# Ninth key blocks of two P V products multiplied together in 64x64 tiles, with a newly written order of the work

## The chip, the cores and the metric

The kernel runs on one core of a Trainium2 chip. The metric is the device time of one execution in microseconds; three runs of the kernel before took 446.49, 446.68 and 447.13 us, and the median, 446.68, is the time that the change is measured against.

## What is computed

Attention with a threshold, over 8 batches of 8 heads with 576 positions of 64 numbers, and then a feed-forward layer on the 4608 tokens:

```python
scores = scale * q @ k.T                          # per batch and head, 576 x 576
thresh = max(scores, axis=-1) - tau               # tau = 0.02
scores = where(scores >= thresh, scores, -1e9)
attn   = exp(scores - max(scores)); attn /= sum(attn) + 1e-9
x      = (attn @ v), heads side by side           # 4608 x 512
h      = maximum(x @ w1, x @ w2, x @ w3)          # 4608 x 768
out    = h @ w_out                                # 4608 x 512
```

All inputs and outputs are fp32.

## The kernel before

**Tiles.** Four heads of a batch make a quad; there are 16 quads. Within a quad, r = 0 and 1 are its two pairs of heads, and i the head within a pair. A head's 576 positions are cut into four blocks of 128 and a rest of 64. The rests of the two heads of a pair share one chunk, so a quad has nine chunks of 128 queries, and a chunk has two score tiles of 128 x 576, one for each pair. The steps (g, idx) are numbered in the order in which they are worked; batch 7 is split in two parts (SPLIT, line 36), so that its feed-forward layer can begin after the first 256 positions of each head.

**One score tile** goes through these steps, each with a letter:

- S (`scores`, line 287): fp32 matmuls of q and k into a PSUM slot. For the fifth chunk of a quad they are of 64x64 tiles, else of 64x128.
- m (`maximum`): VectorE finds the row maximum. For a *masked* tile (its digit in MASKED, line 24, is 1) it also copies the negated scores to SBUF, so that the slot is free afterwards.
- e (`exponents`): ScalarE. For a masked tile exp, from SBUF; for others a Prelu from PSUM that flattens what lies under the threshold, and frees the slot.
- k or n (`numerators`): the second pass with the row sum, on VectorE (k, comparing and multiplying, two operands in SBUF) for masked tiles, on ScalarE (n, exp) for the others.
- r: the reciprocal of both sums of a chunk, on VectorE; p (twice a chunk): the normalisation to bf16 on GpSimd (POOL in the profile), tile P; t: a transposing DMA on SyncE's queue, which brings P into the quad's tile ptq, keys on the partitions.

**The product P V** (O, `product`, line 366) is made per quad and pair r. Its output is a PSUM slot in which head i of the pair has the partitions 64i to 64i + 63. Five key blocks are summed up: four of 128 keys with V's tile vb, and the ninth one, in which the 64 remaining keys of pair 0 stand on partitions 0 to 63 and those of pair 1 on partitions 64 to 127. To multiply that block over all 128 partitions, the tile vrb (`vrs`, line 219, named vr in the profile) has zeros on the other pair's partitions; six memsets put them there at the start. All products are thus 128x64 tiles, the two heads beside each other in the array. A row of 576 queries is written in two runs, of 512 and 64 columns (each matmul writes within one bank of 512). w (VectorE) or x (ScalarE) copies the sum to the tile xt as bf16. `cast_v` (line 221, letter y, on POOL) makes the bf16 V: one copy of the four blocks and two for the ninth.

**The other work:** T transposes q and k of a later quad on PE, a and c copy them out, q swaps halves on POOL; F and B are the two halves of a feed-forward step on PE, h and v (hidden layer) and u (output) its copies on ScalarE and VectorE, o the store; l loads q, k, v of a later quad, g and z load and cast weights.

**The order is written by hand:** the string ORDER (line 40) holds one letter for each step, and S, T, O and F carry the number of the PSUM slot (0 to 3, two banks each) that they take. `issue` (line 603) reads it. Every engine and SyncE's DMA queue work in the order in which their letters stand; between engines only data and free buffers decide.

Of the kernel before, what the change touches and what calls it, by code (L numbers as in the profile page):

```python
# [12 lines left out]
BF16 = mybir.dt.bfloat16  # L13
AX = mybir.AxisListType.X
AF = bass_rust.ActivationFunctionType
# [6 lines left out]
FLAT = 2.0 ** -100  # L22

MASKED = """
010100101001000000011101001010000001100010001000101000011000100000100000
000011111001100001001001001001000001011100101001000110001010010000010011
000010011101100001001100100001001010001100010111000001000100000110000101
001001001101100000110001000100100100001100100011100111010011010111110110
"""


# [6 lines left out]
PBUFS = 6  # L38

ORDER = """  # L40
lllllmlyelgS2ymylS3emgnlT0mleS1lakS2nlqermS3ylmeS0pmeS1kpS3elmS2nlzmelrmnT1pS0tcnperkT1pameS1zmteS3knpS0rnmp
emS2permeqS1mnqT3meqktepS0ncS2ntrpmS3npretprmeS1pmnS0tpmS3npmS1etpmeS0rT2mnplkeT1akgeS2qmgepmteS3rkpekntS0pe
rrnmT2pncS3ptamepS1meqtrS2meyqnS3lmqeS0pmelpknT1lpS2nmeymeS3lrkepS0tcnT2rpnmS1tpnmaprrmS0eS2pmteS1pmT3epctep
meT3O0ykntnyS2etrykpnO1wnprmaS0xptrS3meS2zmeS1mzgeS0mlnS3pmleS1pmelO2qmelpkteO0nrnklpS3nlwgxprrmS2leS0pmeF3q
tmT1eBqcF0eqkthBpnS2vS1nF3pmnF0pmBerBkepS2vhT1tnprmS0S3apmetS1zmeS2rmpeF3tmF0epBkepF1tnBvBznvS2ghS3rymnF0gmS
1eplBrkepF2tnmF3BnpvBnqvT1S0hprrcT2S3pamS1eymzF2emBeqgkF0etyS3nS1vpnmtF2pBmezBveS3prgnS0mtS1phrmT3epO2metzeF
0wpnS1gcqS2nmBqnmO3zekepgS1xvlF2nS3mtnF0rrmpBeBlpveS1lphS2mntF3zmeBrpS0evS1lpnmF2lnpS3rmleBptmS1nzvS0nS3mtpn
S2rpeF1rmepmtepS0mBepmtekF3ektekT2uBarklpukS0uqlS2urS1mlnS3pmleO0pmlepmelO2wtnkS1xrS0tepmF2myF3eBkepT1tBhcF0
nqvT2T1laByrcynS3qvS2nlqmF1tnpF0meS3pBelmBlhrrF2kpelS1vnBlprF3mnlS0pveBtprmS1hS2pmeS3tpmeS0pmF2emF1eBkeT3Bva
tF0nvqT2T3BkqlaS1nrcS3phmtS2npmF0epF1mteBqkBeqF3lnvS2lnBrvplS0hmtpS1F3meS2mteBrmepS0vnpO1rekpnO3mtnpweS2yrrt  # L50
xS1mF0yymT3epBcnS1pvS2nptF3meS0pmeBomT2hS1okeF0omF3ntBkaBervS1ponrF2vpemS0ptuS3mpeF2metknT1T3rknBparrceS0puS
3mqtuS1mpeS2mpeS3lmF0peomepS1ketqT3S2ncBqnmlqnmlO3ekluktO1urnwperrS0pxS3mptnS2mS1pempS3etmF0peF2meBlkBelS1kh
oF3nrmlF0pnBtvpBerrvS2phlS1mnpS3tmF0peS2mpeBmeF3vF1eoBkntS0vnBS2rmhpS3mepS1mteyF2mF0eyBkteBnrvT3pF1aovT2ynBp
lrcS3hplS0mnyF2lmF1elBykepBlnvT3tS0aS2vnO3rrmtpnmpeS1weptS2mS0prmO3eqtmeqF1eqlT0S2xqcBnlpmS3hlpS0meF2ymF1elB
knlF3vnBokBetS2hvS0nrrF3mpF1mpeBkBpetF2vnprS0uvnT3ptmS2aS1pmeS0trmF3epmnpkeS2tS0ermpBnmopnkS1uS2rurompS0eF3o
mpelmpeS2lkpeS0lmS1elqBmelqmetkO2unktO0erwpurkpT1txT2cS3apF0nmtT1qS2ceBqmnS1yF3hmF2eyrBpeBvptnF0pS1vnBrmtpS3
hS2pmeS0mtS1eF3meF2meBkBeF0knF1vnBBrvhpS3nvT0pF2akyF1tnBmyS0velByrmlS3phS2rlempF1lmyeF0pklBepS3tnvS2nBrmptO1
meprvepS2wnS3plmF0nF1rmepBlkeqS2lBhmtT3nyS0vnS2mqlO1emtpecT2xT0rS3pacF1eqmF2lnyBklqeT0BvlaS3khoS1qnmF0tF2pme
BrBopnvS3teprvF0pnrmS1puS2meS3prmS0epF1tmepmepT2ktBeqncT3tuS0kaS2urqmS3tnpmS1nF0pmemteS3repS1mS2lepmBelykteS
3kuO1rumplnmlpO0ewterpT2xS1cqnoS3mpF0nF2metBkeBkF1hlF3nvBlnrrS0pvlnBpmS2lhS1ymleF0mtS3epBmepF2vF1etkBnS0vnS3  # L60
rmBnpS2rhmpF0emF1pteBkpBerF3vnS2ptvnT0pBramS1pthS0mepF3meqtT2rBecpS1nvylT0ynS2pmlS3amlS1eomS0elO2rmpeomeplO3
ketnwT1F0nctF2xkBnBrvpS1hrF3pmS0qBemqS2onvF1yeF0mBopkeF3tyBnS2vqhBrlrnmpT1S0vaptS2empF1S3mpelBkeplF0vntS2rum
S1pnS0mtepF3rmepmetqS2kS0epBnmmteS1rkepS2lmuS0ulpmS1nlymT3yetF2cekeT3oBrknpamoS0npS3mnS1qtmuO0qurrmqelO2wpel
kpelS0xS3meptF2mS1peBemytF0hrkT3pBecF2nS1vpnS3rymtBpnmS0epS1vlnF3mF2etBmeBkhF0lkeF3nBrvpS1nrvBpnS2mptS0hmpeS
3meF2tmF1eBkeBlrvnT0plS3ravlpS2nlmqF0nlS1mqeBtrrmpF2eS3phBlmepS0tvepS1mS2npS3mepO0meknO1meownT3orxkT2pS0tacF
1nF2qrmeBtpS3evpBmS0tyhF1meT2yBcqoeF3rpkT2F0aptBnvBnS2pvS1hqtmF3nqT0meBrS1npvF2npmT3BactS1ervF3prmS0pueS2omp
F3ekqelmT1ntS0qcnBpmekteS2S1urrmpF0uompekS3eptS2nmS1pnmlO3ermtpekO2pnwS1ykxtyS3emS2BomeyrmepS1rukpS2uoF3meF0
opmnBtykBhpS1ervS2eptmO3pO0mxnS3txS2rmepF0empF1ekBtBevF3hkS2nS0mnBrmF1npF2vepBkBtS0hvO3emO2xkS1xerS3rpmF2mpF
0eF1kpteBnBvpF3BvtBrhkpF2S0vS1prmBptmF3eF0pveBtBhS1vS2mS3mF0F1mBkBF2vhF3keBeO0vnO1kF2kxeBwurS1rvpS0mpS2F3mpe
tmpeS0eoF1mnketBknkBurrupoF2puF0hptF3uvF2pvF1hF0tvF3rvpF2hF1vopF0vF3thF2vF1vF0hoF3vF2ovF1hF0vF3vO2uoO1wF0xF3  # L70
F2hF1vF3vF2hF1vF3vF2hF1vF3vF2hF1vF3vF2hF1vF3vF2hF1vBvF3uuooBF2uuuooo
"""


# [28 lines left out]
def kernel(  # L103
# [34 lines left out]
    one = ctx.enter_context(tc.tile_pool(name="one", bufs=1))  # L138
# [30 lines left out]
    vp = ctx.enter_context(tc.tile_pool(name="vp", bufs=3))  # L169
# [196 lines left out]
    def product(L, r, target, part=None):  # L366

        pt, vb, vrb = L["pt"], L["vb"], L["vrb"]
        st = {}

        runs = {None: ((0, 640, 0, 512), (512, 576, 512, 64)),
                1: ((0, 640, 0, 256),),
                2: ((256, 896, 0, 256), (512, 576, 256, 64))}[part]

        order = [(m, run) for m in range(5) for run in runs] if part is None else \
            [(m, run) for run in runs for m in range(5)]

        def first(where):
            st["ps"] = ps = bank("o", where)
            for m, (*q0, p0, n) in order:  # L380
                for i in range(2):
                    w = vb[:, 2 * r + i, (1, 3, 0, 2)[m], :] if m < 4 else vrb[:, 2 * r + i, :]
                    tensor.matmul(ps[64 * i:64 * i + 64, p0:p0 + n], w,
                                  pt[:, 4 if m == 4 else m + 5 * r, q0[i]:q0[i] + n],
                                  start=(m == 0), stop=(m == 4))

        def on_vector():
            ps = st["ps"]
            dst = target(L["b"])[:, 2 * L["qd"] + r, :]
            if part is None:  # L390
                vector.tensor_copy(out=dst, in_=ps[:, 0:S])
            else:
                vector.tensor_copy(out=dst[:, 256:S], in_=ps[:, 0:320])

        def on_scalar():
            ps = st["ps"]
            dst = target(L["b"])[:, 2 * L["qd"] + r, :]
            if part is None:
                scalar.activation(out=dst, in_=ps[:, 0:S], func=AF.Copy)
            elif part == 1:  # L400
                scalar.activation(out=dst[:, 0:256], in_=ps[:, 0:256], func=AF.Copy)
            else:
                scalar.activation(out=dst[:, 256:S], in_=ps[:, 0:320], func=AF.Copy)
        p = _Piece((L["b"], L["qd"], r, part), first)
        p.vector = on_vector if part != 1 and r == 0 else None
        p.scalar = on_scalar if part == 1 or r == 1 else None
        return p


# [177 lines left out]
    def tiles():  # L587
# [8 lines left out]
    line = {k: [] for k in "menkrptahvuxwcq"}  # L596
# [116 lines left out]
    x = 0  # L713
# [39 lines left out]
```

## Time and profile before

| | |
|---|---|
| runs | 446.49, 446.68, 447.13 us |
| span of the profiled execution, first to last instruction | 445.0 us |
| median of the runs less that span | 1.7 us |
| PE (matmuls) busy, of the span | 95% |
| VectorE (DVE) | 88% |
| ScalarE (ACT) | 89% |
| GpSimd (POOL) | 71% |
| mean TensorE clock granted | 0.992 |
| score tiles, masked ones among them | 288, 105 |

The profile gives no time of its own for the profiled execution beside its span; the 1.7 us are what lies around the span when it is set against the median. In the profile's rows, L91 is the line of the helper that records every operation, so operations are told apart by engine, tile and shape: `o<-ptq,vb 128*64 128x512` is a product's matmul, in an array tile of 128 rows and 64 columns, with 128 x 512 moving numbers. PEld is the loading of weights. Matmul ends are modelled, so the starts carry more than the lengths. SPq is SyncE's DMA queue. "by line" rows are shares of a stretch in the chain of waits.

### The profile page before, as it was taken

What the parts mean: (1) busy time and instruction counts of PE and PEld (TensorE: products, weight loads), DVE (VectorE), ACT (ScalarE), POOL (GpSimd) and SP (SyncE); (2) the same over time, 40 slices, a digit from 0 to 9 for tenths busy, and PEclk for the clock granted to TensorE, in tenths of its full rate; (3) what the DMA queues carried; (4) which work ended last, traced back from release to release, by engine and by line L of the source; (5) the groups of instructions that cost most, each with busy time, mean ns of one, the idle gap of its engine ahead of it and who ended that gap; (6) DMA issues with size and microseconds to landing.
All of it is one profiled execution on the core that took longest, in us unless ns stands there. A gap on an engine that the chain in (4) does not pass through costs nothing.

```text
span 445.0 us, 14089 instructions
## 1 busy us (share of the span) xinstructions
PE 423.6 (95%) x5193; PEld 313.3 (70%) x5193; DVE 393.2 (88%) x1093; ACT 394.4 (89%) x804; POOL 315.9 (71%) x422
## 2 busy tenths in 40 slices
PE   7767799999999999999999999999999999999995
PEld 5434557767787767777687867867687778777772
DVE  4989889999999999989989998999999999989641
ACT  4999999999999999999998999999999999956422
POOL 3998989989686686686768885859767789562300
PEclk9998899999999999999999999999999999999999
DMA  8989999999999978999797999899999979882902
GB/s 251 331 162 213 243 195 234 221 245 229 215 255 195 250 165 175 234 187 228 179 223 170 200 224 182 211 234 199 197 220 202 253 121 173 148 122 34 217 13 108
DMA packets 212773, 87.44 MB, mean 196 GB/s; under 512 B 185824, under 2 KB 199648, under 8 KB 212704
## 3 DMA queue, kind: packets, MB, share of 16 engines
q1 hardware_dynamic: 212000, 85.69, 93.6%
q10 hardware_dynamic: 704, 0.85, 0.6%
q8 instruction: 41, 0.67, 0.6%
q14 instruction: 28, 0.23, 0.2%
HBM read 34.60 MB, written 9.44 MB: 99 GB/s over the span
## 4 chain that ended last, share of the span: by engine, by line
PE 81%; ACT 7%; DVE 6%; issue 4%; POOL 2%; DMA 1%; DVEq 0%; POOLq 0%; ACTq 0%
PE ph L91 30%; PE sc L91 28%; PE po L91 11%; PE o L91 8%; ACT z L91 6%; PE tp L91 4%; DVE z L91 2%; DVE unused L91 2%; DMA qm<-in_q_dram 1%; POOL P L91 1%; DVE hm L91 0%; POOL w L91 0%; ACT qt L91 0%; POOL qs L91 0%; DVE hT L91 0%
## 5 line engine op out<-in xcount | busy, mean ns | idle before, releaser
L91 POOL TENSOR_SCALAR P<-z,rs 128x576 bf16<-128x576 f32 x288 | 228.1, 807 | 85.7 <-DVE rs L91 36.4
L91 PE MATMUL sc<-kt,qt 64*128 64x320 f32 (+2 forms) x640 | 179.1, 429 | 4.9 <-ACT z L91 4.4
L91 PE MATMUL sc<-kt,qs 64*128 64x256 f32 (+2 forms) x640 | 178.6, 418 | 4.7 <-ACT z L91 2.7
L91 PE MATMUL ph<-xt,w 64*128 64x288 bf16 (+2 forms) x2160 | 163.9, 283 | 0.3
L91 PEld LDWEIGHTS <-w 64*128 64x128 bf16 (+1 forms) x2160 | 124.8, 94 | 30.9 <-issue 5.3
L91 DVE TENSOR_SCALAR_CACHE_REDUCE unused<-sc 128x576 bf16<-128x576 f32 x183 | 133.2, 749 | 8.9 <-PE sc L91 8.4
L91 ACT ACTIVATE z<-sc,nm 128x576 f32<-128x576 f32 x183 | 131.3, 740 | 8.5 <-DVE unused L91 5.2
L91 ACT ACTIVATE z<-z 128x576 f32<-128x576 f32 x183 | 123.5, 680 | 0.1
L91 PEld LDWEIGHTS sc<-kt,qs 64*128 64x128 f32 (+1 forms) x640 | 92.4, 178 | 25.3 <-ACT z L91 8.1
L91 PEld LDWEIGHTS sc<-kt,qt 64*128 64x128 f32 (+1 forms) x640 | 92.4, 178 | 19.8 <-ACT z L91 9.3
L91 DVE SCALAR_TENSOR_TENSOR z<-z 128x576 f32<-128x576 f32 x105 | 84.1, 811 | 0.4 <-ACT z L91 0.4
L91 DVE TENSOR_SCALAR_CACHE_REDUCE z<-sc 128x576 f32<-128x576 f32 x105 | 77.7, 752 | 7.4 <-PE sc L91 3.4
L91 ACT ACTIVATE z<-z,nm 128x576 f32<-128x576 f32 x105 | 79.1, 773 | 3.6 <-DVE z L91 3.2
L91 POOL COPY qs<-qt 64x640 f32<-64x640 f32 (+3 forms) x68 | 47.0, 692 | 14.4 <-ACT qt L91 11.0
L91 PE MATMUL po<-wo,hT 64*128 64x512 bf16 (+1 forms) x480 | 54.0, 356 | 0.1
L91 DVE TENSOR_TENSOR hm<-ph,hm 128x576 bf16<-128x576 f32 (+2 forms) x54 | 37.0, 686 | 13.0 <-PE ph L91 11.8
L91 ACT ACTIVATE hm<-ph 128x576 bf16<-128x576 f32 (+2 forms) x54 | 32.1, 594 | 18.4 <-PE ph L91 18.1
L91 PEld LDWEIGHTS <-hT 64*128 64x128 bf16 (+1 forms) x480 | 29.6, 97 | 17.1 <-issue 2.9
L91 DVE TENSOR_TENSOR hT<-ph,hm 128x576 bf16<-128x576 f32 (+2 forms) x54 | 37.2, 688 | 3.1 <-PE ph L91 0.6
L91 PE MATMUL o<-ptq,vb 128*64 128x64 bf16 (+2 forms) x544 | 38.7, 282 | 0.0
L91 ACT ACTIVATION_READ_ACCUMULATOR z<-z 128x1 f32 x183 | 36.2, 198 | 0.0
L91 PEld LDWEIGHTS <-vb 128*64 128x64 bf16 x544 | 22.6, 111 | 15.1 <-issue 6.8
(32 smaller groups left out, 274.2 us busy)
## 6 DMA issues: line engine op xcount, KB each, us to landing
vm<-in_v_dram SPq DMA_DIRECT2D x32, 256.0 KB, 5.1
out_dram<-ob SPq DMA_DIRECT2D x31, 256.0 KB, 2.8
qm<-in_q_dram SPq DMA_DIRECT2D x15, 512.0 KB, 4.5
km<-in_k_dram SPq DMA_DIRECT2D x15, 512.0 KB, 5.4
stage<-in_moe_w_dram SPq DMA_DIRECT2D x9, 512.0 KB, 5.3
ptq<-P SPq DMA_TRANSPOSE x144, 4.1
stage<-in_moe_w_out_dram SPq DMA_DIRECT2D x3, 512.0 KB, 4.7
qm<-in_q_dram SPq DMA_DIRECT2D x16, 64.0 KB, 2.9
```

The costliest lines, as they stand in the source:

```text
L91: ins = fn(*a, **kw)
```

## The change

The ninth block leaves the product. O now multiplies the four blocks of 128 keys only. A new step N, once for each two products of a quad (or of a quad's part), multiplies the ninth blocks of both: eight matmuls, in array tiles of 64x64, with the row half chosen by the pair r and the column half by the head i. V needs no zeros: vrb is a tile of two column blocks from the pool of vb, cast in one copy, and the memsets are gone. The copies w and x of both products come behind N. In the split batch's second part the product now keeps its columns at 256 to 575 of the slot instead of 0 to 319.

ORDER and MASKED are written anew. ORDER has 18 N's more and 16 y's fewer; all other steps occur as often as before, but k and n: MASKED has 129 ones for 105, so 24 tiles take the path with k. By batch the ones are 12, 9, 13, 14, 13, 12, 12, 20 before and 16, 13, 15, 15, 16, 13, 16, 25 after. Two O's of a quad stood with other PE steps between them in four of 18 cases, now in two.

```diff
-    vrs = [one.tile([128, 4, D], BF16, name=f"vr{x}") for x in range(3)]
...
-        L["vrb"] = vrs[(2 * L["b"] + L["qd"]) % 3]
-        for r in range(2):
-            rows = slice(64 * r, 64 * r + 64)
-            pool.tensor_copy(out=L["vrb"][rows, 2 * r:2 * r + 2], in_=L["vr"][rows])
-            yield
+        L["vrb"] = vp.tile([128, 2, D], BF16, name="vrb")
+        pool.tensor_copy(out=L["vrb"], in_=L["vr"])
+        yield
...
-                2: ((256, 896, 0, 256), (512, 576, 256, 64))}[part]
+                2: ((256, 896, 256, 256), (512, 576, 512, 64))}[part]
...
             for m, (*q0, p0, n) in order:
                 for i in range(2):
-                    w = vb[:, 2 * r + i, (1, 3, 0, 2)[m], :] if m < 4 else vrb[:, 2 * r + i, :]
-                    tensor.matmul(ps[64 * i:64 * i + 64, p0:p0 + n], w,
-                                  pt[:, 4 if m == 4 else m + 5 * r, q0[i]:q0[i] + n],
-                                  start=(m == 0), stop=(m == 4))
+                    tensor.matmul(ps[64 * i:64 * i + 64, p0:p0 + n], vb[:, 2 * r + i, (1, 3, 0, 2)[m], :],
+                                  pt[:, m + 5 * r, q0[i]:q0[i] + n], start=(m == 0), stop=False)
+
+        def ninths(run):
+            *q0, p0, n = run
+            rows = slice(64 * r, 64 * r + 64)
+            for i in range(2):
+                tensor.matmul(st["ps"][64 * i:64 * i + 64, p0:p0 + n], vrb[rows, i, :],
+                              pt[rows, 4, q0[i]:q0[i] + n], start=False, stop=True)
...
-    for t in vrs:
-        for x in range(2):
-            vector.memset(t[64 - 64 * x:128 - 64 * x, 2 * x:2 * x + 2, :], 0.0)
...
         elif what == "O":
             p = next(todo["O"])
             p.first(where)
-            for k, fn in (("x", p.scalar), ("w", p.vector)):
-                if fn:
-                    line[k].append(fn)
+            line["N"].append(p)
+        elif what == "N":
+            both = [line["N"].pop(0) for _ in range(2)]
+            for run in both[0].runs:
+                for p in both:
+                    p.ninths(run)
+            for p in both:
+                for k, fn in (("x", p.scalar), ("w", p.vector)):
+                    if fn:
+                        line[k].append(fn)
```

The strings MASKED and ORDER, replaced as a whole, are left out of the diff here. One line of the written order near the end, with the last two products (O), reads before and after:

```
tmpeS0eoF1mnketBknkBurrupoF2puF0hptF3uvF2pvF1hF0tvF3rvpF2hF1vopF0vF3thF2vF1vF0hoF3vF2ovF1hF0vF3vO2uoO1wF0xF3
eS1F3F0tpBBukuF3mehrF1eF2F3kvrF1pvhnktoF2uvpF3hF1vrF2F3vF1vhF2vF3pvpF1F2uhppvvpF0hF3vF1F2tottoO0uO3NvF1xwF2F
```

More of the change, by code (lines that the diff above doesn't have):

```diff
@@ L24 @@
 MASKED = """
[L25 to L28, printed above, removed]
+100101100110010001010110001100010101011010001001001001011000100001011000
+001011110110100001000011001010010001001101101110000110001010010000111000
+110011010111000001011100001000011010010010101110100001000100001110000010
+011100011101100000110001010101000101101100010111100111110011110111111101
 """
@@ L46 @@
[L46 to L55, printed above, removed]
@@ new lines @@
+eBkF3T2cBeS1hS0nvnF2memrzzpltqkptleeF3pptlllBnlBhgS1tgvmS0tS2nT3rS1apmS3emF2mnemryepkF1eeBvF0BrkBS2S3hF0npqp
+vlmemS1ppmBnvF2rT1BcvezkqzS0F3T1BmnnepprS2maS1hF3tgemeF0BepS2kvpS1nF3ngtBrmepBmnvpyhS1rtS2F0emmrS3ptpzzpmBen
+T2vS1S3cmmleenO0pqqkO2eektNrS1xglwlnS3mpF2zmreF0BBvpkS1epmhS2mntgrlF3S0pynemptltpBF2vS1BmteretzllpS3pvS0nS1F
+2menmrmenyT3aeeS0S1BkmS3rpppmkkmeS1puqF0uerpenS2S3mBekmekmrS1ukmpplutnteO2rkO0lNwexppnS3S1tlpyrmF0eF2mekpBhn
+tT3BF1cT0tpqtrvaqT3BS2cpqF0nnS3vmBeF1S2mhBerkF0tS3omeplvnpBF1mneS2lolBvyrmrS0mphS3pmS1epS0lmemeeF2F3BkeBT1F0
@@ new lines @@
+nvaT2vcnBpyhrkyppqT3S1aS2F0S3mF1rmBnmltenpenBkeF3S2vvBmS0pptqqmkF1ohS3BmrtevtpeS2tS0nO3meneO1rpqmkeNS2wplmpF
+0lT3cxS1tlneBF3rmpS2nrvpeBS1lttmrlmhekenF0pS3BS2meF1pvmF3T0BkrppyvS2punpmaeS3mneT0qF1S3T2enBcrS0aS2kqutllrtu
+omkeypppS3mS1mmmrS2eopmeS0F3peemT1ttkcneBeS2krS1uknltmmlutkprnpeqpO0O3qpNexwS2plrnmS1S0S3F2mF1eeBppmmrltBptk
+tlelhS0envF2mnF3tlkBlBtoS1rveS0S2hF3pnrmmpmS1BpmvekepF2F0BS3eneBtlvmnS1S2plthnmrrmS0eleF1pF3tmkpeBeBF2npvT0T
+1aBvrhkS3S0F2lcnlrF1pmmBppvnpeBeS3vnT2rmaS0npeqS1S2mqpmeS3ermmO0epO1NeF2pkxkwT3cBS1nqmyhenF0pkS3BtqmrlF2vnS1
@@ new lines @@
+reBmF3S0evBphmF1T2ttBlS3aeF2kvkmprnF1otBlltoypplS0rtuoS1veS3mS2neF0mmpprmS1kS2pBeeepnmeumkpuS3rmpS2mS1mS0F3p
+eeS2kmkrtypeltttmptpooneBetrullS1lO0kmuO3epyNneT2S1kxnwT3F0caqrT2rpncBS3hmqqqnF2mtrS0BplplmF3pyeS1Bpvpemveen
+S2S0meF1S3mmBS2hF0peF1meBkvBeF3tltnT2BF0vS1aF2BkrpknmhpyerknpqF3BS1nvBS0rvhpS2mmeeF3S0meBppF1mrvnpS2enBmF3rv
+tottelS0tBmhS1pF2kS3BnemppqmlvnreS1S0T3O2cO3enmNpemrpT0wS1kxT3caF2T0meaBvF3rlS0pqpnqBpqehkmS2F1mpS3otlllBmtr
+elF2F0peveBS1S3nuknvmqnmkrS0mF2eeptpS3rnT1lBmcS3rkeppttuoltT0utlaS1ppS2mpnmF0eqS1metS2kremS3BpnS1epemrmeuukS
@@ L372, in product @@
                 1: ((0, 640, 0, 256),),
-                2: ((256, 896, 0, 256), (512, 576, 256, 64))}[part]
-        order = [(m, run) for m in range(5) for run in runs] if part is None else \
-            [(m, run) for run in runs for m in range(5)]
+                2: ((256, 896, 256, 256), (512, 576, 512, 64))}[part]
+        order = [(m, run) for m in range(4) for run in runs] if part is None else \
+            [(m, run) for run in runs for m in range(4)]
         def first(where):
@@ L392, in on_vector @@
             else:
-                vector.tensor_copy(out=dst[:, 256:S], in_=ps[:, 0:320])
+                vector.tensor_copy(out=dst[:, 256:S], in_=ps[:, 256:S])
         def on_scalar():
@@ L402, in on_scalar @@
             else:
-                scalar.activation(out=dst[:, 256:S], in_=ps[:, 0:320], func=AF.Copy)
+                scalar.activation(out=dst[:, 256:S], in_=ps[:, 256:S], func=AF.Copy)
         p = _Piece((L["b"], L["qd"], r, part), first)
@@ L406, in product @@
         p.scalar = on_scalar if part == 1 or r == 1 else None
+        p.runs, p.ninths = runs, ninths
         return p
@@ L595 @@
                 O=products(), F=pieces())
-    line = {k: [] for k in "menkrptahvuxwcq"}
+    line = {k: [] for k in "menkrptahvuxwcqN"}
     casts = iter([w[1] for w in wl])
```

36 lines of the change are left out of this document (15 added, 21 removed).

## The prediction

> **What bounds the kernel now.** I read the page first: its span and engines, and its chain of the work that ended last.
>
> ```profile
> span 445.0 us, 14089 instructions
> PE 423.6 (95%) x5193; PEld 313.3 (70%) x5193; DVE 393.2 (88%) x1093; ACT 394.4 (89%) x804; POOL 315.9 (71%) x422
> PE 81%; ACT 7%; DVE 6%; issue 4%; POOL 2%; DMA 1%; DVEq 0%; POOLq 0%; ACTq 0%
> ```
>
> Three engines are at 88 to 95%, so a share of the whole says little. I cut the span by busy time, into the fill, the stretch in which attention has no feed-forward work beside it yet, the long middle, and the end.
>
> ```profile
> 0.00:20.00 20.00, 14.02 (x139) 9.91 (x139) 13.00 (x39) 14.06 (x29) 12.65 (x24) 1.00 0.93 294
> 20.00:80.00 60.00, 49.53 (x488) 32.77 (x490) 54.23 (x161) 58.79 (x123) 54.84 (x71) 0.94 1.09 210
> 80.00:410.00 330.00, 329.57 (x4279) 250.24 (x4278) 311.03 (x858) 308.81 (x627) 244.04 (x323) 1.00 0.98 197
> 410.00:445.00 35.00, 30.53 (x295) 20.40 (x290) 14.93 (x37) 12.76 (x29) 4.38 (x7) 0.99 0.47 114
> ```
>
> The columns after the length are PE, PEld, DVE, ACT and POOL. From 20 to 80 us ScalarE is busy 58.79 of 60 us: it bounds there, with VectorE 4.6 us behind it. From 80 to 410 PE has no gap left, while DVE has 19.0 us and ACT 21.2 us free. The chain of waits, asked for these two stretches, says the same:
>
> ```profile
> by line: ACT z L91 28.9%; issue 19.5%; DVE z L91 10.7%; PE sc L91 9.5%; PE ph L91 6.8%; DVE unused L91 5.8%; POOL P L91 5.0%; POOL w L91 3.4%; PE tp L91 2.4%; POOL qs L91 2.1%; DVE kt L91 1.3%; DVE hT L91 1.3%; ACT qt L91 1.2%; DVE hm L91 1
> by line: PE sc L91 35.3%; PE ph L91 34.0%; PE po L91 11.3%; PE o L91 10.8%; PE tp L91 4.3%; DVE unused L91 1.2%; issue 1.1%; ACT z L91 0.5%; DVE z L91 0.4%; DVE hm L91 0.4%; DVE hT L91 0.2%; DVE kt L91 0.2%; DVE rs L91 0.1%; DVEq L91 0.0%;
> ```
>
> In the first (20:80) ScalarE's z leads; in the second (80:410) PE's own lines make 95.7%. So PE work removed after 80 us comes off the span nearly one for one, and before 80 us it is worth nothing.
>
> **The change part by part.** *The ninth blocks.* PE's timeline at two products that follow each other (start, length, instruction, count):
>
> ```profile
> 115.00 0.43 PE L91 MATMUL sc<-kt,qs 64*128 64x320 f32 x1
> 115.27 0.43 PE L91 MATMUL sc<-kt,qs 64*128 64x320 f32 x1
> ...
> 115.82 0.43 PE L91 MATMUL sc<-kt,qs 64*128 64x320 f32 x1
> 116.18 1.18 PE L91 MATMUL o<-ptq,vb 128*64 128x512 bf16 x16
> 117.19 0.41 PE L91 MATMUL o<-ptq,vr 128*64 128x512 bf16 x4
> 117.44 1.16 PE L91 MATMUL o<-ptq,vb 128*64 128x512 bf16 x16
> 118.43 0.41 PE L91 MATMUL o<-ptq,vr 128*64 128x512 bf16 x4
> 118.78 0.53 PE L91 MATMUL sc<-kt,qt 64*128 64x320 f32 x1
> ```
>
> The ends are modelled, so I go by starts. The four ninth-block matmuls take 117.44 - 117.19 = 0.25 us of the array, like any other key block; a quad's two products pay 0.50. Where the tile shape changes something is added: a score pass of 320 columns is followed by the next on its half after 0.27 us (115.00 to 115.27), but by the first 128x64 product after 0.36 (115.82 to 116.18), and out of the products it is 118.78 - 118.43 - 0.25 = 0.10. One change of shape costs 0.09 us. The new step N issues eight 64x64 matmuls, four of 512 columns and four of 64. If four run at once it streams what one ninth block streamed, 0.25 us. That four do run at once is shown by fp32 scores of fifth query chunks, whose two tiles are sixteen 64x64 matmuls (the count has two more that began before):
>
> ```profile
> 106.93:108.06 1.13, 1.13 (x18) 1.00 0.71 162
> ```
>
> 1.13 less one switch of 0.09 is 0.52 us a tile for eight matmuls, no more than an ordinary tile's two passes of 0.27 for four. So a full quad saves 0.50 - 0.25 = 0.25 us, fourteen of them 3.5 us. The split batch's two quads save a little four times:
>
> ```profile
> 423.17 0.28 PE L91 MATMUL o<-ptq,vr 128*64 128x256 bf16 x2
> 423.27 0.29 PE L91 MATMUL o<-ptq,vb 128*64 128x64 bf16 x8
> ```
>
> 0.10 us for 256 columns, and at most 0.13 with 64 more: 0.5 us together. Against that I counted the changes of shape along the two written orders, by each PE step's tile shape: 91 before, 105 after (18 steps into N, less four because two pairs of products no longer have other work between them). Fourteen times 0.09 is 1.3 us. PE work falls by 3.5 + 0.5 - 1.3 = 2.7 us, of which two quads (0.16 each) lie before 80 us: **-2.4 us**.
>
> The trace has no eight weight loads of 64 columns within 0.25 us, so N lies between 0.25 and 0.50 us (one row half after the other); I take 0.25, as the fp32 tiles are the nearest row. The Trainium skill, page "TensorE: Matmul & The Clock Gate", section "LDWEIGHTS (loading the stationary operand)", gives a load as its columns over 1.2 ns, which I make 53 ns each; eight in line would be an estimated 0.43 us and the saving 2.5 us less. No row here shows such a line.
>
> *What waits longer.* Both products' PSUM slots are held until N, so the first copy out (w on DVE) comes about 1.3 us later. In the new order the step behind N takes another slot in all 18 places.
>
> ```profile
> L91 DVE CAST xt<-o 128x576 bf16<-128x576 f32 x14 | 10.5, 750 | 0.6 <-PE o L91 0.5
> ```
>
> It costs between nothing and one such copy each where the next steps on PE are short; I take 0, since the other two slots cover it.
>
> *The masks.* MASKED has 105 ones before and 129 after; by batch (36 digits each) +4, +4, +1, +2, +3, +1, +4, +5. A one moves a score tile's second pass from ACT (n) to DVE (k). Two timelines show where the next instruction can start, and a group of the page the mean of all k:
>
> ```profile
> 202.59 0.75 DVE L91 SCALAR_TENSOR_TENSOR z<-z 128x576 f32<-128x576 f32 x1
> 203.27 0.08 DVE L91 DVE_READ_ACCUMULATOR z<-z 128x1 f32 x1
> ```
>
> ```profile
> 202.02 0.67 ACT L91 ACTIVATE z<-z 128x576 f32<-128x576 f32 x1
> 202.59 0.19 ACT L91 ACTIVATION_READ_ACCUMULATOR z<-z 128x1 f32 x1
> 202.68 0.73 ACT L91 ACTIVATE z<-sc,nm 128x576 f32<-128x576 f32 x1
> ```
>
> ```profile
> L91 DVE SCALAR_TENSOR_TENSOR z<-z 128x576 f32<-128x576 f32 x105 | 84.1, 811 | 0.4 <-ACT z L91 0.4
> ```
>
> By starts DVE gains 0.68 us and ACT loses 0.66. The mean of 811 ns against the undisturbed 0.75 says that some k are held up, 0.06 on average: 0.74 us. For 24 tiles DVE gets 17.8 us more and ACT 15.8 less. Six of them belong to the first three quads, whose tiles make the stretch to 80 us: there ACT falls by 4.0 to 54.8 and DVE rises by 4.4 to 58.7. The bound changes engines and hardly moves: by these sums 0.1 us less, while by dense starts (0.68) 0.5 us less. The range is from -4 (all of ACT's relief) to +3 (the two engines, both near full, hold each other up); I take **-0.5**.
>
> Eighteen fall after 80 us: DVE 311.0 + 13.3 = 324.4 of some 328. Its 19.0 us of idle time there must shrink to about 4. Who it waited for:
>
> ```profile
> DVE unused L91 <- PE sc L91: 5.5, 14, 0.9
> DVE z L91 <- PE sc L91: 2.8, 8, 0.7
> DVE hm L91 <- PE ph L91: 2.2, 6, 0.7
> DVE kt L91 <- PE tp L91: 1.7, 2, 1.0
> ```
>
> These 12.2 us are waits for PE, which vanish when DVE runs late, and each wait also lets the instruction ahead of it count 0.07 longer (0.75 instead of 0.68). ACT has run at 98% from 20 to 80, so 99% is not out of reach, but little slack is left. Bounds 0 and the 9.5 us of half the idle time kept; I take **+0.7**, near the lower end, because the waits are for PE.
>
> *Small things.* DVE's six memsets of V's padding (in the fill, before DVE has data) go: 0, ACT and PE end that stretch. POOL casts the ninth V block in one copy for two; POOL has 86 us free in the middle: 0.
>
> *The end.* The last products need the last chunk's sums, two normalisations and the transposing DMA; beside them run the first half's eighteen feed-forward steps:
>
> ```profile
> 414.09 8.03 PE L91 MATMUL ph<-xt,w 128*128 128x256 bf16 x72
> ...
> 416.89 0.15 DVE L91 RECIPROCAL rs<-sm 128x2 f32<-128x2 f32 x1
> 417.20 1.46 POOL L91 TENSOR_SCALAR P<-z,rs 128x576 bf16<-128x576 f32 x2 [0.94 <-POOL P L91]
> 418.69 1.31 SPq L91 DMA_TRANSPOSE ptq<-P  x1
> 422.73 0.60 PE L91 MATMUL o<-ptq,vb 128*64 128x256 bf16 x8
> ```
>
> ```profile
> DMA to landing us min/median/max: 3.2/4.1/8.3
> ```
>
> The products start 4.04 us after the DMA's issue, and the median landing is 4.1: no slack. In the new order there are 11 F steps (8.03 / 18 = 0.45 us each) between the last r and these products where there were 12, and five P where there were two. So PE may wait 0 to 0.45 + 3 x 0.73 = 2.6 us; I take **+0.5**, for one F step, since POOL takes a P as soon as its r is there.
>
> The sum on the profiled span: 445.0 - 2.4 - 0.5 + 0.7 + 0.5 = 443.3 us. The median of the runs, 446.68, is 1.7 above that span; the forecast is **445.0 us**, 0.4% faster.
>
> **The rivals.** *A, the forecast:* 442.5 to 447.
>
> *B, VectorE becomes the bound of the middle (slower).* It decides once DVE keeps more than 330 - 324.4 = 5.6 us of its 19.0 us of idle time. With half of it (9.5) the stretch takes 333.9, +3.9 where I have -1.7: 445.0 + 5.6 = **450.6**; with 40% **448.7**. For it: the added k's lie thick, and k is the DVE operation that is held up. Against it: most of the idle time is waiting for PE, and a masked tile frees its score slot after DVE, without waiting for ACT. The Trainium skill, page "SBUF — State Buffer", section "SBUF: two separate sides", lets VectorE with two SBUF inputs and GpSimd exclude each other for whole instructions; k and P are such a pair, and with POOL busy 71% and half a P of 0.73 still to run, an estimated 0.26 us for each k, 6 us in all, would follow. The row of the k's mean shows 0.06.
>
> *C, the row halves do not overlap in bf16 (the change does not do what it says).* N costs 0.50: 14 x 0.25 = 3.5 us more, **448.5**. Against it stand the fp32 tiles.
>
> *D, the end loses what the ninths save:* all five P stand ahead of the last transpose, 2.2 us more: **447.2**.
>
> *E, ScalarE's relief counts in full* before 80 us, and DVE costs nothing: 445.0 - 3.5 - 0.7 = **440.8**.
>
> **How the numbers follow.** A 0.46, B 0.30, C 0.07, D 0.10, E 0.07. A measurement of this kernel tells about 0.2% (0.9 us) from no change. A and E give faster 0.46 (A's upper tail of 0.07 is within 0.2%), D and the near end of B the rest of "same": faster 0.46, same 0.16, slower 0.38. Likely cases of both signs hold most of the chance: A's own range is 442.5 to 447, and the whole range 441.0 to 450.5 leaves out half of E and the far part of B.
>
> **What would show it.** Right: the o group's ninth part at 64*64, four starts within 0.02 us and 0.25 us to the next; 0.09 us ahead of it; DVE about 411 us busy and ACT about 379; PE's lines still above 93% of the chain from 80 to 410; no gap before the last products. Wrong: waits of PE for DVE ("PEld sc <- DVE") of several us in the middle (B), 64*64 starts 0.2 us apart (C), PE idle near 420 us waiting for a DMA (D). What would upset the sum most is DVE's middle, its term of +0.7.

## The result, and the profile after

Four runs of the changed kernel have a median of 462.44 us (461.49 to 464.29), four of the kernel before on the same chip 446.90. The ratio is 1.035, with a 95% interval of 1.0318 to 1.0383: **15.5 us slower**, where 0.4% faster was forecast, and outside the range given. The profiled execution took 464.29 us, 1.8 more than its span, and is the longest of the four, so places are read from it, and sums from medians. One run of all the experiments, 607.13 us at a granted clock of 0.656 (ninths between the products, old order), is left out of every ratio, but counted in that kernel's median of 446.97.

The page's span, engines and chain:

```profile
span 462.5 us, 14061 instructions
PE 431.9 (93%) x5193; PEld 307.4 (66%) x5193; DVE 415.6 (90%) x1135; ACT 383.0 (83%) x756; POOL 327.4 (71%) x406
PE 31%; DVE 9%; issue 3%; DMA 2%; POOL 2%; ACT 1%; SPq 0%; DVEq 0%; POOLq 0%
```

The shares of the chain make only 48%, so it reaches back no further than about 240 us, and nothing is built on it. DVE and ACT are near the 411 and 379 us that were forecast. Busy time by stretch, cut as before:

```profile
20.00:80.00 60.00, 47.33 (x424) 28.12 (x422) 55.44 (x158) 51.60 (x104) 55.48 (x66) 0.89 0.99 221
80.00:410.00 330.00, 321.20 (x4095) 235.00 (x4097) 315.38 (x861) 297.14 (x586) 245.95 (x303) 0.99 0.96 191
410.00:445.00 35.00, 34.56 (x430) 25.33 (x427) 26.33 (x73) 15.90 (x31) 13.78 (x16) 1.00 0.66 137
```

From 20 to 80 us no engine is at its limit any more: ACT, busy 58.79 before, has 8.4 us free. From 80 to 410 PE has 8.8 us of gaps where it had 0.4, and does less of its work there (4095 instructions for 4279). DVE is busy 315.38, not the 324.4 that the forecast needed: **14.6 of its 330 us stay idle**. The rest of the work is pushed behind 410 us.

Who waits for whom over the whole span (engine, tile, who it waited for: us in all, times, longest), after and then before:

```profile
ACT z L91 <- DVE z L91: 13.4, 22, 1.3
ACT z L91 <- DVE unused L91: 10.5, 18, 1.5
PEld sc L91 <- DVE z L91: 9.8, 21, 1.1
DVE z L91 <- POOL P L91: 9.5, 13, 4.0
```

```profile
ACT z L91 <- DVE unused L91: 5.2, 15, 0.7
PEld sc L91 <- DVE z L91: 4.9, 13, 0.7
DVE z L91 <- POOL P L91: 3.3, 6, 1.3
ACT z L91 <- DVE z L91: 3.2, 6, 1.8
```

VectorE's row maxima (tiles z and unused) come later, ScalarE waits for them 23.9 us instead of 8.4, and score slots open later for TensorE. VectorE itself waits three times as long for a z buffer that GpSimd's P has to free.

The ninth blocks themselves do what was forecast. TensorE's timeline at the first N behind 128 us:

```profile
127.31 1.18 PE L91 MATMUL o<-ptq,vb 128*64 128x512 bf16 x16 [0.35 <-ACT ob L91]
128.41 0.44 PE L91 MATMUL o<-ptq,vrb 64*64 64x512 bf16 x8
128.78 0.53 PE L91 MATMUL sc<-kt,qt 64*128 64x320 f32 x1
```

In the single starts the four of 512 columns begin at 128.413 to 128.423, the four of 64 at 128.653 to 128.663. From N to the next scores is 0.37 us: 0.27 of work and one change of tile shape, 0.095.

**Where the time is lost** is seen by measuring each quad from its first row maximum to that of the next quad, in five traces and in that of before (us more than there; the last column ends with the span; the other four kernels are experiments below):

```
quad                0    1    2    3    4    5    6    7    8    9   10   11   12   13   14  15+end
after             0.5  0.7  2.6  0.4  6.2  0.6  0.1  1.5 -0.1 -0.1  1.5 -0.4 -0.5  2.2  0.6  1.6
order and masks   0.6  0.8  3.3  0.6  2.9  0.3  0.4  1.5 -0.1 -0.0  1.5 -0.4 -0.6  2.2  0.5  2.7
more k, old order 0.9  0.6  1.0  0.6  2.0  1.8  0.2  0.7  1.0  1.5  0.0  1.2 -0.0  1.2  0.0  0.9
fewer k, new ord. 1.0 -0.7  3.7  0.9  3.4  0.6  0.3  1.6 -0.0 -0.2  0.9  0.3  0.4  2.8  0.0  1.9
N between, old o. 1.0 -0.8  0.3 -0.2  0.2  0.0 -0.0  0.0 -0.0  0.0 -0.0  0.0  0.1  0.0  0.0  0.4
```

The quads' losses in the changed kernel make 17.4 us, of the span's 17.5. They sit in quads 2 and 4, in 7, 10 and 13, and at the end. Quad 4's 6.2 holds one wait that can be followed through four views. GpSimd's timeline, SyncE's queue, TensorE's timeline and the busy table (its columns as above, the granted clock third from the end):

```profile
103.46 0.74 POOL L91 TENSOR_SCALAR P<-z,rs 128x576 bf16<-128x576 f32 x1
108.54 1.04 POOL L91 CAST wo<-stage 128x1024 bf16<-128x1024 f32 x1 [4.34 <-DMA stage<-in_moe_w_out_dram]
```

```profile
99.48 1.49 SPq L91 DMA_TRANSPOSE ptq<-P  x1
101.08 0.57 SPq L91 DMA_DIRECT2D stage<-in_moe_w_out_dram  x1
```

```profile
111.87 0.40 PE L91 MATMUL ph<-xt,w 64*128 64x288 bf16 x3 [3.86 <-DVE z L91]
```

```profile
108.00:112.00 4.00, 0.14 (x4) 0.12 (x4) 0.95 (x4) 0.89 (x2) 3.46 (x5) 1.00 1.12 361
112.00:116.00 4.00, 4.00 (x30) 3.47 (x28) 3.55 (x9) 3.47 (x7) 4.00 (x6) 0.59 1.20 289
```

The weight load is issued at 101.08 behind a transpose. Its cast stands at the head of GpSimd's queue 4.34 us, with P's behind it. z buffers stay taken, VectorE stops, then TensorE for 3.86 us, and for the 4 us that follow the granted clock is 0.59. The Trainium skill, page "TensorE: Matmul & The Clock Gate", section "What's actually happening", says that the clock falls to half after an idle window of about 3.4 us and returns after a busy one; these two rows agree. With this order and masks and no N, and with N between the products (experiments below), the same wait took 1.2 and 1.6 us and quad 4 lost 2.9 and 3.0, so about half of the 6.2 may belong to this execution alone; the three shorter runs of the changed kernel have no trace.

### The profile page after: what moved, and what is told of

The parts are those of the page before. It is cut to its first block, busy times and chain, and to the rows that moved or that the text cites. A ratio compares the mean times of both kernels' runs of the same rounds, so it can differ in the third digit from the quotient of the medians.

```text
span 462.5 us, 14061 instructions
## 1 busy us (share of the span) xinstructions
PE 431.9 (93%) x5193; PEld 307.4 (66%) x5193; DVE 415.6 (90%) x1135; ACT 383.0 (83%) x756; POOL 327.4 (71%) x406
## 5 line engine op out<-in xcount | busy, mean ns | idle before, releaser
L91 POOL TENSOR_SCALAR P<-z,rs 128x576 bf16<-128x576 f32 x288 | 241.7, 852 | 90.5 <-DVE rs L91 42.0
L91 PE MATMUL sc<-kt,qt 64*128 64x320 f32 (+2 forms) x640 | 185.9, 437 | 6.9 <-ACT z L91 3.4
L91 PE MATMUL sc<-kt,qs 64*128 64x256 f32 (+2 forms) x640 | 184.6, 426 | 5.3 <-POOL qs L91 2.4
L91 PE MATMUL ph<-xt,w 64*128 64x288 bf16 (+2 forms) x2160 | 171.7, 284 | 5.6 <-DVE z L91 4.3
L91 ACT ACTIVATE z<-sc,nm 128x576 f32<-128x576 f32 x159 | 115.1, 738 | 21.0 <-DVE unused L91 10.5
L91 DVE TENSOR_SCALAR_CACHE_REDUCE unused<-sc 128x576 bf16<-128x576 f32 x159 | 116.7, 748 | 2.6 <-PE sc L91 1.9
L91 DVE SCALAR_TENSOR_TENSOR z<-z 128x576 f32<-128x576 f32 x129 | 111.7, 873 | 0.4 <-ACT z L91 0.3
L91 PEld LDWEIGHTS sc<-kt,qs 64*128 64x128 f32 (+1 forms) x640 | 92.2, 181 | 26.3 <-ACT z L91 5.5
L91 ACT ACTIVATE z<-z,nm 128x576 f32<-128x576 f32 x129 | 97.0, 771 | 13.8 <-DVE z L91 13.4
L91 ACT ACTIVATE z<-z 128x576 f32<-128x576 f32 x159 | 107.5, 679 | 0.4
L91 DVE TENSOR_SCALAR_CACHE_REDUCE z<-sc 128x576 f32<-128x576 f32 x129 | 95.3, 749 | 12.5 <-POOL P L91 9.5
L91 ACT ACTIVATE hm<-ph 128x576 bf16<-128x576 f32 (+2 forms) x54 | 32.1, 595 | 17.5 <-PE ph L91 16.9
```

What stands on the lines that cost most here:

```text
L91: ins = fn(*a, **kw)
```

## The experiments

The theory at first: the ninths save what was forecast, and **the new order places waits at the heads of queues** (with VectorE's added load making them worse). The rivals: **the held slots** cost it, or **VectorE's load** does, or the 64x64 products do. Each ratio, with its 95% interval in brackets, is to runs of the kernel before on the same chip, whose medians were 446.46 to 448.00 us.

### The two halves of the change, apart

Ninths alone keep the old order and masks: N behind each second O, w and x behind N, three pairs of products that stood apart put together:

```diff
-...hrmT3epO2metzeF0wpnS1gcqS2nmBqnmO3zekepgS1x...
+...hrmT3epmetzeF0pnS1gcqS2nmBqnmeO1O3NwzkepgS1x...
```

> The ninths in 64x64 tiles (N, V without padding) in the order and with the 105 masks of before; three products stand elsewhere so that both slots can be held until N. If the newly written order or the masks cost the 15.5 us, this is PE's saving alone: 14 x 0.25 less 18 switches of 0.09, some 444 to 445.5 us, at most 447. If holding both products' slots until N, or 64x64 tiles one after the other, is the cause, it is above 455.

462.31 us, 1.0366 [1.0329, 1.0402]: the order theory's 444 to 445.5 was missed by 17 us. VectorE and ScalarE now wait for the products (1.4 and 2.5 us before):

```profile
DVE xt L91 <- PE o L91: 18.9, 14, 3.5
ACT xt L91 <- PE o L91: 7.7, 7, 2.7
```

Order and masks alone, with the code of before, the N's taken out and V's third cast put back:

> The new order and the 129 masks with the ninth blocks as before (inside each product, V padded; no N). If order or masks are the cause: 463 to 466 us, a little above the changed kernel, since PE has 2.7 us more work. If the ninths are the cause: 446 to 450.

464.46, 1.0398 [1.0354, 1.0442]: the new order and masks cost all of the loss without any 64x64 product. Adding the ninths to them (the changed kernel) takes 2.1 us off, in line with the 2.4 forecast, but the intervals overlap.

The masks alone in the old order, and the old masks in the new order (k and n swapped where the digit differs, which is at 86 tiles, 55 one way and 31 the other; 42 e's moved up in the second, since a slot is then freed by another step):

> The kernel before with the 129 masks; where a tile changes its path, k stands where n stood, nothing else moves. If VectorE's load is the cause (24 more k, each held up by P): 455 to 462 us, DVE above 412 busy. If the order of the queues is the cause: 446 to 449.

> The changed kernel with the 105 masks of before in the new order (n where k stood, and 42 of the e's moved ahead because an unmasked tile holds its slot until e). If VectorE's load is the cause: 446 to 451 us. If the order of the queues is the cause: 458 to 464, with POOL's wait of 4 us for the weights near 104 us still there.

490.77 (1.0995 [1.0979, 1.1011]) and 493.17 (1.1049 [1.1025, 1.1072]). Both are far worse than either kernel, so they say only that each order was fitted to its masks: a digit moves the step that frees a slot, and the steps behind are written for it. Load cannot be told from place in this way.

### The held slots and the joint products

The order of the first run with the product of before, without N: the slots are held nearly as long (to the second O), the three pairs stand together.

> The kernel before with its masks and its padded V (no 64x64 products), but in the order of the run of ninths alone: the first product of three quads moved next to the second, and each product's copy out of PSUM behind the quad's second product, so that both slots are held as long as a joint ninth would need. If the 16 us of the run of ninths alone came from the held slots and the three gathered pairs: 462 to 467, with VectorE's wait for the products near 19 us and the same three stretches long. If they came from the 64x64 products or their change of tile shape: 446 to 450.

453.0, 1.0101 [1.007, 1.0133]: between the two expectations. The three gathered pairs lose 1.8, 1.7 and 2.7 us in their quads, and the rest of the order nothing. Each product's own ninths in 64x64 tiles, in the old order:

```diff
             p.first(where)
-            line["N"].append(p)
+            for run in p.runs:
+                p.ninths(run)
+            for k, fn in (("x", p.scalar), ("w", p.vector)):
+                if fn:
+                    line[k].append(fn)
```

> The changed kernel's code, but each product does its own ninths in 64x64 tiles directly behind its four blocks and is copied out at once; order and masks of before (one of three letters for V's cast dropped, since there are two casts a quad). No slot is held longer and nothing is saved on TensorE: two changes of tile shape for each of 36 products at 0.09 us each are at most 6.5 us more. If only those count: 448 to 453. If products in 64x64 tiles cost something of their own in the old order: above 457.

452.57, 1.0105 [1.0065, 1.0145], as expected. The count on record was an upper bound; along the written order there are three more changes of shape for each of 14 adjacent pairs of products and two for each of the four other pairs, 50, and 50 x 0.095 = 4.75 us against the 4.6 measured. Copies two instructions of their own engine further back in the run of ninths alone:

> The run of the ninths alone (old order, 105 masks), with the copies w and x moved behind up to two more instructions of their engines, as far as the next use of the slot lets them. If that run lost its time because VectorE stood 18.9 us at w waiting for N, this takes 4 to 10 us off its 462.3. If the loss sits in PE itself (slots held by two products, tile shapes), it stays within 2 us.

467.89, 1.0459 [1.0431, 1.0487]. VectorE's wait for the products did fall to 9.8 us, but the slots were held longer: TensorE's scores waited 6.2 us for VectorE's copies (3.2 in the run of ninths alone), and their weight loads 4.1 us for ScalarE's (1.3). Then hold and wait were taken away together. The joint ninths go **between** the two products, closing the first and opening the second; order, masks and padded V are those of before, and the three pairs that stand furthest apart keep their own ninths, so 15 pairs take part:

```diff
         def first(where):
             st["ps"] = ps = bank("o", where)
+            if not joint:
+                return blocks(ps, range(5))
+            if opens:
+                for run in runs:
+                    last[0](run)
+                    ninths(ps, run, True)
+            else:
+                last[0] = lambda run: ninths(ps, run, False)
+            blocks(ps, range(4))
```

> The kernel before, its order and masks untouched, its padded V kept, with the joint ninths of a quad in 64x64 tiles between the two products: the first product's four blocks, the joint ninths that close it and open the second, then the second's four blocks. Nothing is held longer than before. The three pairs that stand apart multiply their ninths as before. On TensorE each of 15 pairs gives 0.50 us and takes 0.27 and two more changes of tile shape of 0.095 each, so 0.04 us a pair is saved. If the 16 us of the run of ninths alone came from the held slots and from copies that wait for both products: 445.5 to 448.5. If joint 64x64 products disturb the old order wherever they stand: above 452.

446.97, 1.0006 [0.9989, 1.0022]: no difference.

```profile
116.63 1.18 PE L92 MATMUL o<-ptq,vb 128*64 128x512 bf16 x16
117.74 0.44 PE L92 MATMUL o<-ptq,vr 64*64 64x512 bf16 x8
118.11 1.18 PE L92 MATMUL o<-ptq,vb 128*64 128x512 bf16 x16
```

So joint 64x64 products do no harm, and the run of ninths alone was slow through N's place. Of its 16 us some 6 go with the three gathered pairs, which cost that without N too and stay apart here. The rest goes with w and x at the heads of their queues behind N, where VectorE waits 18.9 us for products against 6.6 in the run without N; the hold and the late copies were not taken away one by one. The same place in the new order, for all 18 pairs:

> The changed kernel with its order and masks, its joint ninths moved between the two products in the same way for all 18 pairs, so that the first product is finished 1.2 us earlier and the second slot opens with the ninths; one more change of tile shape a pair (1.7 us in all). If held slots and late copies cost the new order too: 458 to 461. If the new order was made for the hold, and its loss lies in its queues and in VectorE's load: 462 to 465.

462.93, 1.0364 [1.0334, 1.0393]. The expectation counted 1.7 us of added changes of shape, and the time rose by 0.5 us, within the intervals. So the hold can cost the new order little: its loss lies elsewhere.

### The places of waits in the new order

Each weight load directly behind the cast that frees its buffer; each transpose directly behind its second p; one weight load earlier and its cast four P's later; and with it two of quad 2's swaps earlier (the order's pieces of the last two):

```diff
-...ptpzzpmBenT2vS1...ektNrS1xglwlnS3mpF2zmreF0...F3S0pynemptltpBF2...
+...ptpzzgpmBenT2vS1...ektNrS1xlwlnS3mpF2mreF0...F3S0pynempztltpBF2...
...
-...S3pmgllplrenpmmelpt...rtlppqqkmpS2...
+...S3pmgllpqlrenpqmmelpt...rtlppkmpS2...
```

> The changed kernel with each weight load g directly behind the cast that frees its buffer in the written order. If POOL's wait of 4.3 us at a weight cast near 104 us (PE idle for 3.9, then slow for some 4 us) is part of the loss: 455 to 457.5. If something else would have stopped PE there anyway: within 2 us of 462.4.

> The changed kernel with each transposing DMA t directly behind its chunk's second P in the written order (9 us of written PE work earlier on average), so that no load or store stands ahead of it on SyncE's queue that need not. If late transposes cost time in the middle and at the end: 457 to 460. If they don't: 461 to 463.5.

> The changed kernel with two letters moved: the load of the eleventh weight piece right behind the cast of the tenth (some 2 us earlier on SP's queue), and the cast of the eleventh behind four more normalizations on GpSimd's queue. If the wait of 4.3 us at the head of GpSimd's queue near 108 us, with TensorE's 3.9 us and the slow clock behind it, is the price of where these two stand: the stretch of the fifth quad falls from 31.6 to 26 to 28 us and the time to 457 to 459.5. If the delay only moves on (VectorE behind anyway by its greater load): 461 to 463.

> The run of one weight load earlier, and also the last two swaps of the third quad three to four normalizations earlier on GpSimd's queue, where scores waited 2.1 us for them near 50 us. If queue heads price the start too: a further 1.5 to 2.5 us off, the third quad's stretch from 26.3 to about 24. If the start is bound by VectorE and ScalarE together: no more than 0.5 us off, and the P issued later show as waits of VectorE for GpSimd.

With every weight load early: 468.22, 1.0468 [1.0446, 1.049]. Quad 4's stretch fell from 31.6 to 28.0 us, and quad 2's rose from 26.3 to 33.5, since transposes now stood behind a weight load that waited 4.8 us for its buffer (the three that SyncE issues from 51.19 us in the changed kernel come from 57.87) and the products came late:

```profile
ACT xt L91 <- PE o L91: 11.2, 7, 6.9
DVE xt L91 <- PE o L91: 8.9, 4, 6.0
```

With transposes early: 501.98, 1.1226 [1.1201, 1.125]; loads stood behind transposes that waited for P, and GpSimd's casts waited 14.1 us for weights where they had waited 5.4. One load earlier: 462.62, 1.0305 [1.0252, 1.0357], and 462.53, 1.031 [1.0259, 1.036] with the swaps. Neither is told from the changed kernel. In the first one's profiled execution quad 4 came down to 27.8 us and the run was the shortest of its four, 460.11; the other three were 462 to 463. In the first two runs clearing one queue's head moved the wait to another, and in the last two it gained nothing that can be told; the queue theory is not borne out as a theory of single places.

### VectorE's load

k on 448 of 576 columns, in the new order and, as the control, in the old:

```diff
-            vector.scalar_tensor_tensor(out=zn, in0=zn, scalar=thr, in1=zn,
+            vector.scalar_tensor_tensor(out=zn[:, 0:448], in0=zn[:, 0:448], scalar=0.0, in1=zn[:, 0:448],
```

> The changed kernel with k on 448 of the 576 columns and without the threshold (it leaves that part of the masking out): VectorE's load falls by some 15 us to the level of before, the order is untouched. If VectorE's load is what makes the changed kernel slow: 447 to 453. If it is the order of the queues: at most 4 us off, 458 to 462.

> The control for the run with short k in the new order: the kernel before with k on 448 of 576 columns and the scalar 0.0 (the threshold left out and 128 columns untouched, so not the reference's output). VectorE has some 13 us less to do. If VectorE's load is what the new order pays for, the old order gives back much less than the 5.8 us there: 445 to 447. If both orders are equally bound by VectorE: 440 to 443.

456.67, 1.0198 [1.0159, 1.0237], in the new order, 5.8 us less than with full k; 446.75, 0.9986 [0.9967, 1.0005], in the old one. So VectorE's time taken away helps the new order alone; in the old one TensorE has no gap in the middle that it could close. And with VectorE busy 399.3 us and ScalarE 381.4 (393.2 and 394.4 before) the new order still loses 9 us, in the same quads as the changed kernel: quad 2 with 6.3 us, 4, 7, 10, 13 and the end with 1.0 to 1.9 each in the run's trace. The last two runs move the load and leave every release where it was. In the old order 24 of the n, spread evenly, go to VectorE in their places; their slots are freed where they were:

```diff
+            mv = moved(c["g"], c["idx"], r)
-            vector.tensor_scalar(out=unused, in0=c[r], scalar1=tau, scalar2=None,
-                                 op0=OP.subtract, op1=OP.max, accum_out=nm)
+            vector.tensor_scalar(out=unused, in0=c[r], scalar1=-1.0 if mv else tau, scalar2=None,
+                                 op0=OP.mult if mv else OP.subtract, op1=OP.min if mv else OP.max, accum_out=nm)
...
+            if moved(c["g"], c["idx"], r):
+                scalar.activation(out=zn, in_=c[r], func=AF.Exp, bias=c["bias", r], scale=1.0)
+                return
```

> The kernel before with 24 more second steps on VectorE, spread evenly, in the places where ScalarE had them: for these row halves the maximum is taken without tau, the exponent from PSUM as before, and k does the rest, so that every slot is released where it was (the reference's output). VectorE gets 24 times 0.81 us more, ScalarE 24 times 0.9 less: the change's load in the old order. If load on VectorE is the cause of the loss: 453 or more. If it is a third: 449 to 453. If it is only how the new order places its waits: 446 to 448.

461.57, 1.0317 [1.0301, 1.0332]: **14.4 us from 24 second steps alone**, nearly the whole loss of the change. Its page, its two stretches, its waits and its k:

```profile
PE 429.5 (93%) x5193; PEld 313.8 (68%) x5193; DVE 413.4 (90%) x1141; ACT 380.9 (83%) x756; POOL 327.3 (71%) x422
```

```profile
20.00:80.00 60.00, 47.01 (x441) 29.64 (x442) 57.55 (x164) 53.71 (x109) 55.98 (x67) 0.94 0.99 204
80.00:410.00 330.00, 322.19 (x4122) 241.26 (x4118) 315.53 (x870) 294.52 (x583) 249.51 (x320) 1.00 0.96 196
```

```profile
ACT z L98 <- DVE unused L98: 17.2, 28, 1.8
ACT z L98 <- DVE z L98: 8.6, 9, 2.6
PEld sc L98 <- DVE z L98: 8.4, 16, 1.6
DVE unused L98 <- PE sc L98: 7.0, 18, 1.3
DVE z L98 <- PE sc L98: 3.2, 10, 0.5
DVE z L98 <- POOL P L98: 0.4, 1, 0.4
```

```profile
L98 DVE SCALAR_TENSOR_TENSOR z<-z 128x576 f32<-128x576 f32 x129 | 106.8, 842 | 0.4 <-ACT z L98 0.4
```

The busy times and ScalarE's waits are near those of the changed kernel: DVE busy 315.53 of 330 (315.38 there), PE 322.19 (321.20), ScalarE waiting 25.8 us for VectorE (23.9). VectorE waits 0.4 us for P, and k itself 0.4 us for its exponent, so neither of these stops it. Its waits for TensorE's scores stay: 10.2 us, 11.8 before. My reading is that the alternation itself stops it: its k makes the maximum behind it late, then ScalarE's exponent, and with it the slot for TensorE's next scores. The reverse, 24 of the 129 k in the new order moved in place to ScalarE:

> The changed kernel with 24 of its 129 k moved in place to ScalarE, every slot released where it was (in these row halves only the largest score is kept, so not the reference's output): the load of before in the new order. If the load is the cause: 448 to 454. If a third: 455 to 459. If the new order's own places of waits are the cause: 460 or more, since ScalarE gets 24 times 0.9 us on a text made for less.

465.62, 1.0412 [1.0395, 1.0428]: with nearly the load of before (DVE 397.6 us busy, ACT 396.0) the new order is no faster, but 3 us slower than the changed kernel. The load theory's 448 to 454 was missed. Its losses sit in the same quads as the changed kernel's (2, 4, 7, 13), while the run with more k lost a little nearly everywhere.

So there are two causes: the added load, which makes 14.4 us in the old order with every slot released where it was, and the places of the steps in the new order, which leave 9 us with the short k, where VectorE has only 6 us more than before. The run with fewer k gives 18 us for the places, but part of that is ScalarE's added time: VectorE's reciprocals wait 5.5 us for ScalarE from 80 to 410, against 0.2 in the changed kernel. The two causes don't add up (together 464.46 without the ninths). **What stays open** is which steps of the new order make the second: four guesses at single places failed, and the load was moved back evenly, not to the tiles that the old masks chose. Open too is how much of the 14.4 us comes from the load and how much from 24 places that the old order was not written for; that the loss is spread over nearly all quads speaks for the load, but an exchange of equally many k and n, which would change places alone, was not run.

## Why the prediction was wrong

- *The ninth blocks, -2.4 us: right in kind, not resolved in size.* Four 64x64 products start within 0.01 us, 0.24 us ahead of the next; each change of shape costs 0.095. In the new order the ninths bring 2.1 us with overlapping intervals. Rival C did not occur. The estimate from the Trainium skill's load time (page "TensorE: Matmul & The Clock Gate", section "LDWEIGHTS (loading the stationary operand)"), eight loads in line, 0.43 us, did not come about either: the next scores follow after 0.37 us with the change of shape in it, 0.27 without, where 0.25 was taken.
- *What waits longer, 0: right for the new order* (N between the products changes nothing there that can be told); the reason given, that the other two slots cover the hold, was not tested by itself. In the old order a joint step behind both products cost 16 us, some 6 of them with the gathered pairs.
- *The masks after 80 us, +0.7: this is the step that failed.* "I take +0.7, near the lower end, because the waits are for PE", which "vanish when DVE runs late". In the changed kernel those for row maxima did fall, from 8.4 + 3.4 us over the whole span to:

```profile
DVE unused L91 <- PE sc L91: 1.9, 7, 0.4
DVE z L91 <- PE sc L91: 2.5, 7, 0.8
```

  But others took their place there, above all 7.2 us from 80 to 410 for P (0.7 before). And with the load alone, in the run with more k, the four waits of 12.2 us that the prediction lists for that stretch are still 9.8 us:

```profile
DVE unused L98 <- PE sc L98: 4.5, 14, 0.7
DVE z L98 <- PE sc L98: 2.6, 8, 0.5
DVE kt L98 <- PE tp L98: 1.7, 2, 1.0
DVE hm L98 <- PE ph L98: 1.0, 2, 0.7
```

  So a wait for PE is not free time that a later VectorE takes up: a later maximum makes ScalarE wait, and, as I read it, its exponent frees the slot later, TensorE's next scores come later, and VectorE waits again. In these two traces VectorE stopped at 315.4 and 315.5 of 330 us, with 14.5 us idle where 19.0 had been; with N between the products and without N the new order has 317.1 and 318.6, so 11 to 15 us stay, and the closeness of the first two may be chance. The forecast let it use all but about 4. That is rival B, in its mechanism and by its own deciding point of 5.6 us, but beyond its prices, which stopped at half the idle time. With 14.5 us kept its sum is 445.0 + (324.4 + 14.5 - 330) + 1.7 = 455.6, against 461.57 in the run with more k.
- *The start, -0.5: wrong, by 3.0 us in the old order.* With more k alone the first three quads, which the prediction priced here, lost 2.5 us (3.8 in the changed kernel). The two engines' busy times came near the forecast (DVE 57.55 and ACT 53.71 of 60 in that run, 58.7 and 54.8 forecast), but "the bound changes engines and hardly moves" took one engine's bound as exchangeable for another's; "the two engines, both near full, hold each other up" stood as the upper end, +3. With this step the sum is 458.6; the last 3.0 us up to the measured 461.57 are not assigned. The prediction's list of added masks by batch has two entries exchanged (by the digits the third batch gets 2 and the fourth 1); no term rests on them.
- *POOL's small things, 0, and the queues not priced at all.* The weight cast's wait at 108 us stands in the profile with a price of 1.2 to 4.3 us on its queue. Moving it gained nothing that the runs can tell. That the order was written anew was treated as bookkeeping, apart from the end; the run with short k shows 9 us of loss with 6 us more VectorE work than before and 13 less of ScalarE's.
- *The end, +0.5:* the last stretch lost 1.6 us, and TensorE has no gap before the last four products, so the 2.2 us of rival D are not there (the last two of them):

```profile
439.41 0.85 PE L91 MATMUL po<-wo,hT 128*64 128x256 bf16 x12
440.09 1.29 PE L91 MATMUL o<-ptq,vb 128*64 128x256 bf16 x32
```

## What to carry to other kernels

An engine's idle time in a chain that alternates between engines is not free capacity: here VectorE at 94% took up 4.5 us of new work in 330 and handed the rest on as time, though every single wait named another engine. When an order is written out by hand, price a moved step by the order's slack and not by busy sums, and first try the new operation at a place that leaves the old order as it is; such a run (N between the products) told in one go that the new operation was harmless and, by itself, worth nothing that can be measured. No version here is faster than the kernel before by more than the noise. Moving the load at unchanged releases, in both orders, goes some way to tell load from place; an exchange at equal load would be the control.

## What the runs showed of the hardware

**A k that runs beside one of GpSimd's casts is held up most.** VectorE's and GpSimd's timelines of the changed kernel:

```profile
34.51 1.60 DVE L91 SCALAR_TENSOR_TENSOR z<-z 128x576 f32<-128x576 f32 x1
```

```profile
34.46 1.03 POOL L91 CAST w<-stage 128x1024 bf16<-128x1024 f32 x1
```

This k began 0.05 us after the cast and took 1.60 us; the 27 k with no GpSimd instruction beside them took 0.74 to 0.76. The mean of all 129 is

```profile
L91 DVE SCALAR_TENSOR_TENSOR z<-z 128x576 f32<-128x576 f32 x129 | 111.7, 873 | 0.4 <-ACT z L91 0.3
```

or 0.12 us above 0.75, 15.9 us in all, where it was 0.06 and 6.4 us before; 17 k beside a cast make 6.6 of the 15.9. The Trainium skill, page "SBUF — State Buffer", section "SBUF: two separate sides", lets one such instruction wait for the whole of the other. The k beside a cast agrees within 0.13 us: the cast's remaining 0.98 and 0.75 of its own would be 1.73. The mean is half of the 0.26 that the prediction had estimated from it.
